# Rolled TensorE loops with loads counted on GpSimd, in a decode-step kernel (sliding-window attention beside an MLP)

## The chip, the cores and the metric

The kernel runs on one core of a Trainium2 chip. The metric is device time in microseconds (us) of one execution, the median of several runs. All times of the profile are in us from the start of the profiled span, if nothing else is said.

## The reference

One token (batch 1, one position, width 1024) goes through two branches whose results are added to the token. All tensors are bf16.

```python
x  = A_x
xn = layernorm(x)                                   # 1024 values
# A: attention of 32 heads in 4 groups over the last 4096 cached positions
q  = xn @ wq                                        # wq 1024 x 4096
scores = einsum(q, k_cache[:, :, -4096:]) * 128**-0.5
o  = softmax(scores) @ v_cache[:, :, -4096:]
a  = o @ wo                                         # wo 4096 x 1024
# B: MLP
h  = gelu(layernorm(xn) @ w1 + b1)                  # w1 1024 x 3584, tanh form
b  = h @ w2 + b2                                    # w2 3584 x 1024
out = x + a + b
```

Weights and cache together are 38 MB (of 2 to the 20 bytes): K and V 4 each, wq and wo 8 each, w1 and w2 7 each. Each is used once, by a single row of activations, so nearly all of the work is to bring them in.

## The kernel before

**Memory.** Each matrix lies in SBUF with 128 partitions. `WA` holds wq and later w2 and the end of wo; `W1` holds w1 and later most of wo; `KV` holds K and later V; `KT` is K transposed in blocks of 32 x 32 by DVE. So w2 can be loaded once q has been computed, V once K has been transposed, and wo once h has been computed.

**Loads.** SP (SyncE) issues all large transfers in one queue, in this order: four pieces of K (L212), wq in two halves of 4 MB, w1 in two halves of 3.5 MB (L152), then, after a wait on K's last transpose, four pieces of V (L266), after a wait on q (`done["q"]`) w2 in pieces of 16 and 12 rows, and after a wait on h (`done["h"]`) wo. A "row" of w2 or wo is here one matmul step: 128 partitions x 1024 columns, 256 KB. wo has 32 of them, in pieces of 10, 8, 6, 4, 2 and 1, with row 31 apart: eight small transfers (L275) put it into 64 partitions (`LOW`) between the second and the third piece.

**TensorE.** All its products have a single row of activations. The activations are the stationary operand (a window of a mostly zero tile, so that step number n writes into one PSUM row), the weights are the moving operand, 512 columns at a time. In order:

- the two layer norms' broadcast of x (L373);
- q: two loops, one for each half of wq, each with 8 rounds of 4 matmuls (`row_mms`, L379);
- the first half of h: 7 rounds of 4 (L379);
- the scores: 32 matmuls written out (L412), which need `QBD`, the transposed q that DVE makes in the meantime (copy L282, transpose L284, eight small copies L291);
- the second half of h, 7 rounds of 4. Meanwhile DVE and ScalarE make the maxima (L297), exp (L308) and the transposed probabilities (L312);
- h's transposes (L449), then the value product: 4 rounds of 8 (L454). Meanwhile gelu is computed on DVE and ScalarE;
- w2: a loop of 4 rounds of 8 for its first 16 rows (L464), four small matmuls that transpose the attention output (o2, L473), a loop of 3 rounds of 8 for the other 12 rows;
- wo, written out: rows 0 to 23 as pairs of matmuls, each half of the columns on its own 32-column tile of the array (L424); rows 24 to 30 as four matmuls of 256 columns on four tiles side by side (L430).

The first 24 rows' sums stand in two 32-row strips of one PSUM bank; ScalarE moves them (L357) into the bank in which the last rows add up. The two result halves are cast (L363) and written out.

Each loop is `pe.Fori`, a loop that the engine runs itself: addresses that depend on the index are computed by register instructions in TensorE's own instruction stream. For instance:

```python
            for k in rows:
                pe.matmul(bank(n), lhsT=vec[:, bass.ds(t + width * k, 128)], rhs=rhs_at(k, t), start=False, stop=False,
                          skip_group_check=True)
```

Matmul by matmul, one such address is `(index + constant) * 2 + base`.

## Time and profile before

| what | value |
|---|---|
| median of three runs | 101.78 us (100.42, 101.78, 102.19) |
| the profiled execution, its own time | 100.35 us |
| its span in the profile | 99.1 us |
| TensorE: matmuls, weight loads | 70.5 us busy, 341 matmuls |
| DMA read | 39.86 MB, 402 GB/s over the span |
| largest groups | q's 64 matmuls 17.9 us; the four K transposes on DVE 17.4; h's 56 matmuls 13.0; w2's 56 12.5; value product 8.5; scores 7.1 |

In the profile PE is TensorE's matmuls and PEld its weight loads, which run beside them. Register, branch and semaphore instructions are not counted as busy: where TensorE's sequencer works on them, the row says that the idle time ahead of the instruction is due to "issue". "x4" is the number of instructions that were put together in one row; the number in brackets is the idle time of the engine ahead of them, with what ended it. The slices are 2.48 us each, and a digit is the busy share in tenths.

### The profile page before, as it was taken

What the parts mean: (1) busy time and instruction counts of PE and PEld (TensorE: products, weight loads), DVE (VectorE), ACT (ScalarE), POOL (GpSimd) and SP (SyncE); (2) the same over time, 40 slices, a digit from 0 to 9 for tenths busy, and PEclk for the clock granted to TensorE, in tenths of its full rate; (3) what the DMA queues carried; (4) which work ended last, traced back from release to release, by engine and by line L of the source; (5) the groups of instructions that cost most, each with busy time, mean ns of one, the idle gap of its engine ahead of it and who ended that gap; (6) DMA issues with size and microseconds to landing.
All of it is one profiled execution on the core that took longest, in us unless ns stands there. A gap on an engine that the chain in (4) does not pass through costs nothing.

```text
span 99.1 us, 1197 instructions
## 1 busy us (share of the span) xinstructions
PE 70.5 (71%) x341; PEld 28.4 (29%) x341; DVE 37.5 (38%) x56; ACT 5.7 (6%) x11; POOL 6.5 (7%) x26
## 2 busy tenths in 40 slices
PE   0021000305999999999999999799999999979532
PEld 0000000002334433334444344233335445422210
DVE  0007998999999900091002543440024010000001
ACT  0500004200000000000000040000000000000021
POOL 6990000000000000000000000000000000000000
PEclk9999999999999999999999999999999999999996
DMA  2999999999999889889799999998999999999960
GB/s 26 397 426 418 430 436 436 489 476 463 450 423 397 370 382 544 370 382 544 301 423 420 423 522 423 423 423 370 476 476 422 388 397 427 423 402 440 397 256 4
DMA packets 3286, 39.89 MB, mean 402 GB/s; under 512 B 594, under 2 KB 596, under 8 KB 980
## 3 DMA queue, kind: packets, MB, share of 16 engines
q1 hardware_dynamic: 3076, 39.85, 95.0%
q10 hardware_dynamic: 208, 0.01, 0.1%
q8 instruction: 1, 0.02, 0.1%
q14 instruction: 1, 0.01, 0.0%
HBM read 39.86 MB, written 0.00 MB: 402 GB/s over the span
## 4 chain that ended last, share of the span: by engine, by line
DMA 46%; PE 40%; SPq 10%; issue 2%; DVE 0%
PE PS L379 31%; DMA WA<-in_A_wo_dram 26%; DMA WA<-in_A_wq_dram 20%; PE PS L412 7%; SPq L275 6%; SPq L152 2%; SPq L212 2%; PE PS L383 1%; PE PS L436 1%; DVE Pb L363 0%; PE PS L430 0%
## 5 line engine op out<-in xcount | busy, mean ns | idle before, releaser
L379 PE MATMUL PS<-WA,XZ 128*128 x64 | 17.9, 433 | 5.6 <-DMA WA<-in_A_wq_dram 5.2
L261 DVE STREAM_TRANSPOSE KT<-KV 128x4096 bf16<-128x4096 bf16 x4 | 17.4, 4409 | 0.0
L379 PE MATMUL PS<-W,YZ 128*128 x56 | 13.0, 381 | 0.0
L464 PE MATMUL PS<-WA,GT 128*64 x56 | 12.5, 380 | 0.0
L379 PEld LDWEIGHTS PS<-WA,XZ 128*128 x64 | 6.9, 108 | 17.0 <-issue 13.2
L383 PE MATMUL PS<-XBRP,HOT 1*128 1x512 bf16 x6 | 2.5, 454 | 9.5 <-DVE XZ L253 9.5
L454 PE MATMUL PS<-KV,PT 128*128 x32 | 8.5, 378 | 0.7 <-issue 0.7
L464 PEld LDWEIGHTS PS<-WA,GT 128*64 x56 | 6.0, 110 | 5.8 <-issue 1.2
L379 PEld LDWEIGHTS PS<-W,YZ 128*128 x56 | 5.2, 96 | 7.5 <-issue 2.5
L412 PE MATMUL PS<-KT,QBD 128*128 128x512 bf16 x32 | 7.1, 379 | 0.0
L424 PE MATMUL PS<-W,OT 128*32 128x512 bf16 x48 | 5.7, 380 | 1.8 <-DMA W<-in_A_wo_dram 1.8
L363 DVE CAST Pb<-PS 64x256 bf16<-64x256 f32 x1 | 0.4, 417 | 16.1 <-PE PS L430 16.1
L373 PE MATMUL PS<-XBRP,onesb 1*128 1x512 bf16 x2 | 1.0, 605 | 6.7 <-DMA XBRP<-in_B_b_dram 6.7
L297 DVE TENSOR_REDUCE MX<-PS 128x1 f32<-128x512 f32 x2 | 1.4, 692 | 10.0 <-PE PS L412 10.0
L454 PEld LDWEIGHTS PS<-KV,PT 128*128 x32 | 3.1, 96 | 6.1 <-issue 2.7
L223 DVE BATCH_NORM_STATS2 BN<-PS 128x6 f32<-128x512 f32 x2 | 1.3, 688 | 7.7 <-PE PS L373 7.7
L412 PEld LDWEIGHTS PS<-KT,QBD 128*128 128x128 bf16 x32 | 3.1, 98 | 3.7 <-issue 0.2
L383 PEld LDWEIGHTS PS<-XBRP,HOT 1*128 1x128 bf16 x6 | 0.5, 94 | 11.5 <-issue 11.5
L342 DVE SCALAR_TENSOR_TENSOR QBD<-PS,REC,GMASK 32x512 f32<-32x512 f32 x1 | 0.7, 739 | 7.9 <-PE PS L383 7.9
L424 PEld LDWEIGHTS PS<-W,OT 128*32 128x32 bf16 x48 | 2.1, 97 | 5.3 <-DMA W<-in_A_wo_dram 2.8
L282 DVE CAST Pb<-PS 128x512 bf16<-128x512 f32 x1 | 0.7, 692 | 7.4 <-PE PS L383 7.4
L308 ACT ACTIVATE Pb<-PS,NMB 128x1024 bf16<-128x1024 f32 x1 | 1.1, 1114 | 40.1 <-DVE NMB L305 40.1
(79 smaller groups left out, 33.4 us busy)
## 6 DMA issues: line engine op xcount, KB each, us to landing
WA<-in_A_wq_dram SPq DMA_DIRECT2D x2, 4096.0 KB, 24.4
W<-in_B_w_dram SPq DMA_DIRECT2D x2, 3584.0 KB, 41.0
KV<-in_A_k_cache_dram SPq DMA_DIRECT2D x4, 1024.0 KB, 7.9
KV<-in_A_v_cache_dram SPq DMA_DIRECT2D x4, 1024.0 KB, 20.6
WA<-in_B_w_dram SPq DMA_DIRECT2D x1, 4096.0 KB, 27.2
WA<-in_B_w_dram SPq DMA_DIRECT2D x1, 3072.0 KB, 34.2
W<-in_A_wo_dram SPq DMA_DIRECT2D x1, 2560.0 KB, 21.4
W<-in_A_wo_dram SPq DMA_DIRECT2D x1, 2048.0 KB, 25.9
```

What stands on the lines that cost most here:

```text
L152: sp.dma_start(dst[:, c0 * width:(c0 + n) * width].rearrange("p (c n) -> p c n", c=n), src[:, c0:c0 + n, :],).then_inc(semaphores[j], 16)
L212: sp.dma_start(KV[:, g * 4096:(g + 1) * 4096], A_k_cache[0, g, SK - W:SK, :].rearrange("(p i) d -> p (i d)", p=128)).then_inc(s_k[g], 16)
L223: DVE.mark(dve.bn_stats(out=BN[:, 12 * n + 6 * i:12 * n + 6 * i + 6], in_=src[:, 512 * i:512 * i + 512]))
L261: C["kt"] = DVE.mark(dve.transpose(KT[:, i * 4096:(i + 1) * 4096], KV[:, i * 4096:(i + 1) * 4096]))
L275: sp.dma_start(LOW[first:first + 29:4, :].rearrange("p (u n) -> p u n", u=2), low_source[first:first + 29:4]).then_inc(s_low, 16)
L297: DVE.mark(dve.tensor_reduce(out=MX2[:, b:b + 1], in_=S[:, 512 * b:512 * b + 512], axis=AX.X, op=ALU.max))
L379: pe.matmul(bank(n), lhsT=vec[:, bass.ds(t + width * k, 128)], rhs=rhs_at(k, t), start=False, stop=False, skip_group_check=True)
L383: return pe.matmul(bank(n), lhsT=HOT[:, 8:136], rhs=XB[0:1, 0:8, :], start=start, stop=not start, skip_group_check=True)
L412: last = pe.matmul(bank(3 + b), lhsT=QBD[:, g * 512 + j * 128:g * 512 + j * 128 + 128], rhs=K5[:, g, 16 * b:16 * b + 16, j, :], start=(n = ...
L424: ins = pe.matmul(acc(a), lhsT=window(vec, c, a), rhs=rhs[:, a * 512:(a + 1) * 512], start=False, stop=stop, tile_position=(0, 32 * a), sk ...
L454: pe.matmul(bank(1), lhsT=PT[:, bass.ds(i * 256 + u * 32, 128)], rhs=V4[:, :, bass.ds(i * 8 + u, 1), :], start=False, stop=False, skip_gro ...
L464: pe.matmul(bank(7, 64), lhsT=GT[:, bass.ds(i * (4 * STEP) + (LEAD + STEP * (c0 + u) - ROW - a), 64)], rhs=W2[:, bass.ds(i * 4 * D + ((c0 ...
```

## The change

- TensorE's loops are put together: q is one loop over both halves of wq around the loop of 8 rounds; h likewise, and as a whole after the scores; the scores are a loop of 4 rounds of 8; the value product is 8 rounds of 4; w2 is one loop of 7 rounds; wo's first 20 rows are a loop of 5 rounds, through the same code as w2, with matmuls of 128 stationary columns in place of the 64 (w2) and the tiled pairs (wo). [...]
- As one loop's body serves several loads, GpSimd waits for the loads in their order and counts one semaphore, `s_feed`, up; TensorE waits for it against a register, `turn`, that it adds one to in each round.
- w2's and wo's stationary tiles hold each vector twice, 64 columns apart, so that the sums come to stand in rows 31, 32, 95 and 96 of one bank, in which the last 12 rows add up too. ScalarE's move is gone.
- wo's row 31 is loaded as its last piece, not in eight small transfers; the pieces are now 8, 12, 8, 3 and 1 rows.
- K's fourth piece is issued after wq.
- The copy of q is done by ScalarE, and the eight small copies are shared by DVE and ScalarE.
- o2 stands after all of w2.

```diff
-WO_CHUNKS = [10, 8, 6, 4, 2, 1]
-WO_HEAD = 4
+WO_CHUNKS = [8, 12, 8, 3, 1]
+WO_HEAD = 2
-TAIL = 24
+TAIL = 20
+ROUND = 4
...
+    for semaphores, rounds in (
+            (s_wq, [1] * len(WQ_CHUNKS)), (s_w1, [1] * len(W1_CHUNKS)),
+            (s_w2, [n // ROUND for n in W2_CHUNKS]), (s_wo, [n // ROUND for n in WO_CHUNKS[:WO_HEAD]])):
+        for semaphore, n in zip(semaphores, rounds):
+            pool.wait_ge(semaphore, 16)
+            pool.sem_inc(s_feed, n)
...
+    for g in range(3):
+        load_k(g)
     load_chunks(WA, wq_p, WQ_CHUNKS, NQ, s_wq)
+    load_k(3)
     load_chunks(W1, w1_p, W1_CHUNKS, F, s_w1)
...
-    low_source = A_wo.rearrange("(u p j) n -> p u j n", u=2, j=32)[:, :, WO_MAIN, :]
-    for first in (0, 1, 2, 3, 32, 33, 34, 35):
-        sp.dma_start(
-            LOW[first:first + 29:4, :].rearrange("p (u n) -> p u n", u=2),
-            low_source[first:first + 29:4]).then_inc(s_low, 16)
...
-    DVE.mark(dve.tensor_copy(Q32, bank(7)))
+    act.wait_ge(done["q"], 16)
+    C["q32"] = ACT.mark(act.activation(out=Q32, in_=bank(7), func=ACTF.Copy))
...
-        dve.wait_ge(done["sc" if b else "sc0"], 1)
+        dve.wait_ge(done["sc"], 4)
...
-    C["d_GT"] = DVE.mark(dve.tensor_tensor(out=GT[:, LEAD:LEAD + STEP * FC:STEP], in0=HT[:, :], in1=U2[:, :], op=ALU.mult))
+    C["d_GT"] = DVE.mark(dve.tensor_tensor(
+        out=twice(GT, FC), in0=HT[:, :].unsqueeze(1).to_broadcast([128, 2, FC]),
+        in1=U2[:, :].unsqueeze(1).to_broadcast([128, 2, FC]), op=ALU.mult))
...
+    with pe.Fori(0, len(WQ_CHUNKS)) as j:
+        pe.wait_ge(s_feed, turn)
+        pe.reg_add(turn, turn, 1)
+        with pe.Fori(0, 8) as t:
+            for k in range(4):
+                last = add(bank(7), XZ[:, bass.ds(t + j * (4 * XW) + XW * k, 128)],
+                           WA[:, bass.ds(t * -512 + j * (4 * NQ) + (k * NQ + 7 * 512), 512)])
+            last.then_inc(done["q"], 1)
...
+    with pe.Fori(0, 4) as g:
+        for j in range(4):
+            for b in range(2):
+                last = add(bank(3 + b), QBD[:, bass.ds(g * 512 + j * 128, 128)],
+                           K4[:, bass.ds(g * 32 + 16 * b, 16), 32 * j:32 * j + 32])
+        last.then_inc(done["sc"], 1)
+
+    W1C = W1[:, :].rearrange("p (x c) -> p x c", c=4)
+    with pe.Fori(0, len(W1_CHUNKS)) as j:
+        pe.wait_ge(s_feed, turn)
+        pe.reg_add(turn, turn, 1)
+        with pe.Fori(0, 7) as t:
+            for k in range(4):
+                last = add(bank(0), YZ[:, bass.ds(t + j * 32 + 8 * k, 128)],
+                           W1C[:, bass.ds(t + j * F + k * (F // 4), 128, 7), :])
+            last.then_inc(done["h"], 1)
...
+    V3 = V.rearrange("p (g x) -> p g x", g=HKV)
+    with pe.Fori(0, 8) as i:
+        for u in range(4):
+            last = add(bank(1), PT[:, bass.ds(i * 128 + u * 32, 128)], V3[:, :, bass.ds(i * 512 + u * 128, 128)])
+        last.then_inc(done["pv"], 1)
+
+    def out_rounds(vec, weights, rows):
+        with pe.Fori(0, rows // ROUND) as i:
+            pe.wait_ge(s_feed, turn)
+            pe.reg_add(turn, turn, 1)
+            for u in range(ROUND):
+                for a in range(2):
+                    add(bank(7), vec[:, bass.ds(i * (2 * ROUND) + (LEAD + 2 * u - ROW - a), 128)],
+                        weights[:, bass.ds(i * (ROUND * D) + (u * D + a * 512), 512)])
+
     pe.wait_ge(DVE.sem, C["d_GT"])
+    out_rounds(GT, W2, FC)
     pe.wait_ge(DVE.sem, C["on"])
...
+    out_rounds(OT, W1, TAIL)
+
+    c0 = TAIL
+    for j, n in enumerate(WO_CHUNKS[WO_HEAD:]):
+        pe.wait_ge(s_wo[WO_HEAD + j], 16)
+        for c in range(c0, c0 + n):
+            rhs = (W1 if c < FC else WA)[:, c * D:(c + 1) * D]
+            for a in range(4):
+                first, column = LEAD + 2 * c - (0 if a % 2 else ROW), 7 * 512 + a // 2 * 256
+                last = add(PS[32 * a:32 * a + 32, column:column + 256], OT[:, first:first + 32],
+                           rhs[:, TAIL_AT[a]:TAIL_AT[a] + 256], tile_position=(0, 32 * a))
```

More of the change, by code (lines that the diff above doesn't have):

```diff
@@ L23 @@
 W2_CHUNKS = [16, 12]
-WO_CHUNKS = [10, 8, 6, 4, 2, 1]
-WO_HEAD = 4
-WO_LOW = 18
+WO_CHUNKS = [8, 12, 8, 3, 1]
+WO_HEAD = 2
 XW = 136
@@ L29 @@
 XP = 72
-TAIL = 24
+TAIL = 20
 TAIL_AT = [0, 512, 256, 768]
 ROW = 31
-STEP = 2
 LEAD = 32
-GW = 2 * LEAD + STEP * FC
-WO_MAIN = 31
+COPY = 64
+GW = 192
+ROUND = 4
 class Track:
@@ L74, in bass_parallel_sum__sliding_block_cached__mixer_channel_mlp__decode_kernel @@
     s_x, s_b1, s_v, s_out = (nc.alloc_semaphore(n) for n in ("s_x", "s_b1", "s_v", "s_out"))
-    s_low = nc.alloc_semaphore("s_low")
     s_w1 = sems("s_w1", len(W1_CHUNKS))
@@ L85, in bass_parallel_sum__sliding_block_cached__mixer_channel_mlp__decode_kernel @@
     done = {n: nc.alloc_semaphore(f"S_PE_{n}") for n in (
-        "x", "h", "hT", "q", "sc0", "sc", "pv", "tot", "o2", "rest", "fin")}
+        "x", "h", "hT", "q", "sc", "pv", "tot", "o2", "fin")}
+    s_feed = nc.alloc_semaphore("S_FEED")
     def sb(name, shape, d):
@@ L99, in bass_parallel_sum__sliding_block_cached__mixer_channel_mlp__decode_kernel @@
     HOT = sb("HOT", [1, 8 + 128], bf16)
-    EDGE = sb("EDGE", [2, 2 * LEAD + 1], bf16)
+    EDGE = sb("EDGE", [2, 132], bf16)
     XBRP = sb("XBRP", [2, 16 * XP], bf16)
@@ L127, in bass_parallel_sum__sliding_block_cached__mixer_channel_mlp__decode_kernel @@
     ON = sb("ON", [32, DH], bf16)
-    OT = sb("OT", [128, 2 * LEAD + 33], bf16)
+    OT = sb("OT", [128, GW], bf16)
     ONM = QBD[0:32, 0:1024].bitcast(f32)
@@ L132, in bass_parallel_sum__sliding_block_cached__mixer_channel_mlp__decode_kernel @@
     W1 = sb("W1", [128, KC * F], bf16)
-    LOW = KT[0:64, 0:2 * D]
     WA = sb("WA", [128, KC * NQ], bf16)
@@ L191, in bass_parallel_sum__sliding_block_cached__mixer_channel_mlp__decode_kernel @@
         fill=1.0, base=0, channel_multiplier=1))
-    POOL.mark(pool.memset(EDGE[:, LEAD:LEAD + 1], 1.0))
+    POOL.mark(pool.memset(EDGE[:, LEAD:LEAD + COPY + 1:COPY], 1.0))
     POOL.mark(pool.affine_select(
@@ L209, in bass_parallel_sum__sliding_block_cached__mixer_channel_mlp__decode_kernel, with load_k @@
     C["consts"] = POOL.cnt
-    for g in range(HKV):
+    for semaphores, rounds in (
[4 more added lines that the diff above has]
+            pool.sem_inc(s_feed, n)
+    def load_k(g):
         sp.dma_start(
@@ L268, in bass_parallel_sum__sliding_block_cached__mixer_channel_mlp__decode_kernel @@
             A_v_cache[0, g, SK - W:SK, :].rearrange("(p i) d -> p (i d)", p=128)).then_inc(s_v, 16)
-    sp.wait_ge(done["q"], 1)
+    sp.wait_ge(done["q"], 16)
     load_chunks(W2, w2_p, W2_CHUNKS, D, s_w2)
-    sp.wait_ge(done["h"], 1)
-    load_chunks(W1, wo_p, WO_CHUNKS[:2], D, s_wo)
-    low_source = A_wo.rearrange("(u p j) n -> p u j n", u=2, j=32)[:, :, WO_MAIN, :]
-    for first in (0, 1, 2, 3, 32, 33, 34, 35):
-        sp.dma_start(
-            LOW[first:first + 29:4, :].rearrange("p (u n) -> p u n", u=2),
-            low_source[first:first + 29:4]).then_inc(s_low, 16)
-    load_chunks(W1, wo_p, WO_CHUNKS[2:WO_HEAD], D, s_wo[2:], WO_LOW)
-    load_chunks(WA, wo_p, WO_CHUNKS[WO_HEAD:], D, s_wo[WO_HEAD:], FC)
-    dve.wait_ge(done["q"], 1)
-    DVE.mark(dve.tensor_copy(Q32, bank(7)))
+    sp.wait_ge(done["h"], 14)
+    load_chunks(W1, wo_p, WO_CHUNKS[:3], D, s_wo)
+    load_chunks(WA, wo_p, WO_CHUNKS[3:], D, s_wo[3:], FC)
+    act.wait_ge(done["q"], 16)
+    C["q32"] = ACT.mark(act.activation(out=Q32, in_=bank(7), func=ACTF.Copy))
+    dve.wait_ge(ACT.sem, C["q32"])
+    C["qtb"] = DVE.mark(dve.transpose(QTB, Q32))
     dve_wait()
-    DVE.mark(dve.transpose(QTB, Q32))
-    dve_wait()
+    act.wait_ge(DVE.sem, C["qtb"])
     dve.wait_ge(POOL.sem, C["consts"])
+    act.wait_ge(POOL.sem, C["consts"])
     QD = QBD[:, :].rearrange("p (g w) -> p g w", g=HKV)[:, :, 0:512].rearrange("p g (e b h) -> p g e b h", e=4, b=4)
@@ L290, in bass_parallel_sum__sliding_block_cached__mixer_channel_mlp__decode_kernel, with twice @@
         for u in range(2):
-            C["d_QBD"] = DVE.mark(dve.tensor_copy(
-                QD[32 * b:32 * b + 32, :, :, b, 4 * u:4 * u + 4], QS[32 * b:32 * b + 32, u:8:2, :, :]))
+            to, of = QD[32 * b:32 * b + 32, :, :, b, 4 * u:4 * u + 4], QS[32 * b:32 * b + 32, u:8:2, :, :]
+            if b < 2:
+                C["d_QBD"] = DVE.mark(dve.tensor_copy(to, of))
+            else:
+                C["a_QBD"] = ACT.mark(act.activation(out=to, in_=of, func=ACTF.Copy))
+    def twice(vec, n):
+        return vec[:, LEAD:LEAD + 2 * COPY].rearrange("p (u x) -> p u x", u=2)[:, :, 0:2 * n:2]
     S = PS[:, 3 * 512:5 * 512]
     for b in range(2):
-        dve.wait_ge(done["sc" if b else "sc0"], 1)
+        dve.wait_ge(done["sc"], 4)
         DVE.mark(dve.tensor_reduce(out=MX2[:, b:b + 1], in_=S[:, 512 * b:512 * b + 512], axis=AX.X, op=ALU.max))
@@ L312, in bass_parallel_sum__sliding_block_cached__mixer_channel_mlp__decode_kernel @@
     C["d_pt"] = DVE.mark(dve.transpose(PT[:, 0:1024], Pb[:, :]))
-    dve.wait_ge(done["h"], 1)
+    dve.wait_ge(done["h"], 14)
     C["d_h8"] = DVE.mark(dve.tensor_copy(H8, bank(0, 8)))
@@ L319, in bass_parallel_sum__sliding_block_cached__mixer_channel_mlp__decode_kernel @@
         out=HT[:, :].rearrange("p (t c) -> p c t", c=4),
-        in0=PS[:, 6 * 512:6 * 512 + 32].rearrange("p (c t) -> p c t", c=4)[:, :, 0:7],
+        in0=PS[:, 2 * 512 + 32:2 * 512 + 64].rearrange("p (c t) -> p c t", c=4)[:, :, 0:7],
         in1=B1T[:, :].rearrange("p (t c) -> p c t", c=4), op=ALU.add))
@@ L340, in bass_parallel_sum__sliding_block_cached__mixer_channel_mlp__decode_kernel @@
     dve_wait()
-    dve.wait_ge(done["pv"], 1)
+    dve.wait_ge(done["pv"], 8)
     DVE.mark(dve.scalar_tensor_tensor(
@@ L350, in bass_parallel_sum__sliding_block_cached__mixer_channel_mlp__decode_kernel @@
     dve.wait_ge(done["o2"], 1)
-    DVE.mark(dve.tensor_copy(OT[:, LEAD:LEAD + 32], PS[:, 2 * 512:2 * 512 + 32]))
     C["OT"] = DVE.mark(dve.tensor_copy(
-        OT[0:64, LEAD + WO_MAIN + 1:LEAD + WO_MAIN + 2], PS[64:128, 2 * 512 + WO_MAIN:2 * 512 + WO_MAIN + 1]))
-    act.wait_ge(done["rest"], 1)
-    for a in range(2):
-        C["rest"] = ACT.mark(act.activation(
-            out=PS[64 * a:64 * a + 64, 6 * 512:6 * 512 + 256], in_=PS[0:64, 7 * 512 + 256 * a:7 * 512 + 256 * a + 256],
-            func=ACTF.Copy))
+        twice(OT, 32), PS[:, 2 * 512:2 * 512 + 32].unsqueeze(1).to_broadcast([128, 2, 32])))
     for engine, track, a in ((act, ACT, 1), (dve, DVE, 0)):
         engine.wait_ge(done["fin"], 1)
-        of, to = PS[64 * a:64 * a + 64, 6 * 512:6 * 512 + 256], Pb[0:64, 256 * a:256 * a + 256]
+        of, to = PS[64 * a:64 * a + 64, 7 * 512 + 256 * a:7 * 512 + 256 * a + 256], Pb[0:64, 256 * a:256 * a + 256]
         track.mark(act.activation(out=to, in_=of, func=ACTF.Copy) if a else dve.tensor_copy(to, of))
@@ L374, in bass_parallel_sum__sliding_block_cached__mixer_channel_mlp__decode_kernel @@
     last.then_inc(done["x"], 1)
-    def row_mms(n, vec, width, rows, t_count, rhs_at):
-        with pe.Fori(0, t_count) as t:
-            for k in rows:
-                pe.matmul(bank(n), lhsT=vec[:, bass.ds(t + width * k, 128)], rhs=rhs_at(k, t), start=False, stop=False,
-                          skip_group_check=True)
-    def edge(n, start):
-        return pe.matmul(bank(n), lhsT=HOT[:, 8:136], rhs=XB[0:1, 0:8, :], start=start, stop=not start,
-                         skip_group_check=True)
@@ L386, in h_cols, with edge, add @@
-    def h_cols(row, t):
-        return row.rearrange("p (m a c) -> p m a c", m=128, a=7)[:, :, bass.ds(t, 1), :]
+    def edge(n):
+        pe.matmul(bank(n), lhsT=HOT[:, 8:136], rhs=XB[0:1, 0:8, :], start=True, stop=False, skip_group_check=True)
+    def add(to, lhsT, rhs, **place):
+        return pe.matmul(to, lhsT=lhsT, rhs=rhs, start=False, stop=False, skip_group_check=True, **place)
+    turn = pe.alloc_register("turn")
+    pe.reg_mov(turn, 1)
     pe.wait_ge(POOL.sem, C["hot"])
+    for n in (7, 3, 4):
+        edge(n)
@@ L390, in bass_parallel_sum__sliding_block_cached__mixer_channel_mlp__decode_kernel @@
     pe.wait_ge(DVE.sem, C["xz"])
-    edge(0, True)
-    edge(7, True)
+    edge(0)
+    edge(1)
     pe.wait_ge(POOL.sem, C["consts"])
-    k0 = 0
-    for j, n in enumerate(WQ_CHUNKS):
-        pe.wait_ge(s_wq[j], 16)
-        row_mms(7, XZ, XW, range(k0, k0 + n), 8, lambda k, t: WA[:, bass.ds(t * -512 + (k * NQ + 7 * 512), 512)])
-        k0 += n
-    edge(7, False).then_inc(done["q"], 1)
-    def h_rows(j):
-        pe.wait_ge(s_w1[j], 16)
-        k0 = sum(W1_CHUNKS[:j])
-        row_mms(0, YZ, 8, range(k0, k0 + W1_CHUNKS[j]), 7, lambda k, t: h_cols(W1[:, k * F:(k + 1) * F], t))
@@ L406, in bass_parallel_sum__sliding_block_cached__mixer_channel_mlp__decode_kernel @@
-    h_rows(0)
-    pe.wait_ge(DVE.sem, C["d_QBD"])
-    K5 = KT[:, :].rearrange("p (g i j k) -> p g i j k", g=HKV, i=32, j=4)
-    for b in range(2):
-        for n in range(16):
-            g, j = n // 4, n % 4
-            last = pe.matmul(bank(3 + b), lhsT=QBD[:, g * 512 + j * 128:g * 512 + j * 128 + 128],
-                             rhs=K5[:, g, 16 * b:16 * b + 16, j, :], start=(n == 0), stop=(n == 15))
-        last.then_inc(done["sc" if b else "sc0"], 1)
-    def acc(a):
-        return bank(7, 32, 32 * a)
@@ L418, in window @@
-    def window(vec, c, a):
-        first = LEAD + c - (0 if a else ROW)
-        return vec[:, first:first + 32]
-    def out_row(vec, c, rhs, stop=False):
-        for a in range(2):
-            ins = pe.matmul(acc(a), lhsT=window(vec, c, a), rhs=rhs[:, a * 512:(a + 1) * 512],
-                            start=False, stop=stop, tile_position=(0, 32 * a), skip_group_check=True)
-        return ins
-    def tail_row(vec, c, rhs, stop):
-        for a in range(4):
-            ins = pe.matmul(PS[32 * a:32 * a + 32, 6 * 512:6 * 512 + 256], lhsT=window(vec, c, a % 2),
-                            rhs=rhs[:, TAIL_AT[a]:TAIL_AT[a] + 256], start=False, stop=stop, tile_position=(0, 32 * a),
-                            skip_group_check=True)
-        return ins
+    with pe.Fori(0, len(WQ_CHUNKS)) as j:
[6 more added lines that the diff above has]
+            last.then_inc(done["q"], 1)
@@ new lines, in bass_parallel_sum__sliding_block_cached__mixer_channel_mlp__decode_kernel @@
+    pe.wait_ge(DVE.sem, C["d_QBD"])
+    pe.wait_ge(ACT.sem, C["a_QBD"])
+    K4 = KT[:, :].rearrange("p (x k) -> p x k", k=128)
+    with pe.Fori(0, 4) as g:
[13 more added lines that the diff above has]
+            last.then_inc(done["h"], 1)
@@ L435, in bass_parallel_sum__sliding_block_cached__mixer_channel_mlp__decode_kernel @@
+    pe.wait_ge(ACT.sem, C["exp"])
     for a in range(2):
-        pe.matmul(bank(7, 64), lhsT=EDGE[:, 1 - a:1 - a + 64], rhs=XB[:, 8 * a:8 * a + 8, :], start=(a == 0), stop=False,
+        pe.matmul(bank(7), lhsT=EDGE[:, 1 - a:129 - a], rhs=XB[:, 8 * a:8 * a + 8, :], start=(a == 0), stop=False,
                   skip_group_check=True)
-    h_rows(1)
-    edge(0, False).then_inc(done["h"], 1)
-    pe.wait_ge(ACT.sem, C["exp"])
     pe.matmul(PS[0:32, 5 * 512 + 129:5 * 512 + 130], lhsT=B32[:, :], rhs=SUMP[:, :]).then_inc(done["tot"], 1)
-    pe.wait_ge(DVE.sem, C["d_pt"])
@@ L444, in bass_parallel_sum__sliding_block_cached__mixer_channel_mlp__decode_kernel @@
-    pe.wait_ge(s_v, 64)
-    V4 = V.rearrange("p (g i d) -> p g i d", g=HKV, i=32)
     pe.wait_ge(DVE.sem, C["d_h8"])
     for c in range(4):
-        last = pe.matmul(PS[:, 6 * 512 + 8 * c:6 * 512 + 8 * c + 8], lhsT=H8[:, c:512:4], rhs=FLIP[:, :])
+        last = pe.matmul(PS[:, 2 * 512 + 32 + 8 * c:2 * 512 + 40 + 8 * c], lhsT=H8[:, c:512:4], rhs=FLIP[:, :])
     last.then_inc(done["hT"], 1)
-    edge(1, True)
-    with pe.Fori(0, 4) as i:
-        for u in range(8):
-            pe.matmul(bank(1), lhsT=PT[:, bass.ds(i * 256 + u * 32, 128)], rhs=V4[:, :, bass.ds(i * 8 + u, 1), :],
-                      start=False, stop=False, skip_group_check=True)
@@ L456, in bass_parallel_sum__sliding_block_cached__mixer_channel_mlp__decode_kernel @@
-    edge(1, False).then_inc(done["pv"], 1)
-    pe.wait_ge(DVE.sem, C["d_GT"])
-    def w2_loop(j):
-        pe.wait_ge(s_w2[j], 16)
-        c0 = sum(W2_CHUNKS[:j])
-        with pe.Fori(0, W2_CHUNKS[j] // 4) as i:
-            for u in range(4):
-                for a in range(2):
-                    pe.matmul(bank(7, 64),
-                              lhsT=GT[:, bass.ds(i * (4 * STEP) + (LEAD + STEP * (c0 + u) - ROW - a), 64)],
-                              rhs=W2[:, bass.ds(i * 4 * D + ((c0 + u) * D + a * 512), 512)],
-                              start=False, stop=False, skip_group_check=True)
@@ L469, in bass_parallel_sum__sliding_block_cached__mixer_channel_mlp__decode_kernel @@
-    pe.matmul(PS[:, 6 * 512:6 * 512 + 256], lhsT=HOT[:, 8:136], rhs=XB[0:1, 0:4, :], start=True, stop=True)
-    w2_loop(0)
+    pe.wait_ge(s_v, 64)
+    V3 = V.rearrange("p (g x) -> p g x", g=HKV)
[11 more added lines that the diff above has]
+                        weights[:, bass.ds(i * (ROUND * D) + (u * D + a * 512), 512)])
@@ L475, in bass_parallel_sum__sliding_block_cached__mixer_channel_mlp__decode_kernel @@
     last.then_inc(done["o2"], 1)
-    w2_loop(1)
     pe.wait_ge(DVE.sem, C["OT"])
-    c0 = 0
-    for j, n in enumerate(WO_CHUNKS):
-        if c0 == WO_LOW:
-            pe.wait_ge(s_low, 8 * 16)
-            for u in range(2):
-                out_row(OT[0:64, :], WO_MAIN + u, LOW[:, u * D:(u + 1) * D])
-        pe.wait_ge(s_wo[j], 16)
-        if c0 == TAIL:
-            pe.wait_ge(ACT.sem, C["rest"])
+    out_rounds(OT, W1, TAIL)
+    c0 = TAIL
+    for j, n in enumerate(WO_CHUNKS[WO_HEAD:]):
+        pe.wait_ge(s_wo[WO_HEAD + j], 16)
         for c in range(c0, c0 + n):
             rhs = (W1 if c < FC else WA)[:, c * D:(c + 1) * D]
-            last = out_row(OT, c, rhs, c == TAIL - 1) if c < TAIL else tail_row(OT, c, rhs, c == WO_MAIN - 1)
-        if c0 + n == TAIL:
-            last.then_inc(done["rest"], 1)
+            for a in range(4):
+                first, column = LEAD + 2 * c - (0 if a % 2 else ROW), 7 * 512 + a // 2 * 256
+                last = add(PS[32 * a:32 * a + 32, column:column + 256], OT[:, first:first + 32],
+                           rhs[:, TAIL_AT[a]:TAIL_AT[a] + 256], tile_position=(0, 32 * a))
         c0 += n
```

## The prediction, made before the changed kernel ran

> **What bounds the kernel now.** I read the 40 slices first, then the DMA queues, then the order of time around the loops, and last the end of the transfers.

> ```profile
> span 99.1 us, 1197 instructions
> PE 70.5 (71%) x341; PEld 28.4 (29%) x341; DVE 37.5 (38%) x56; ACT 5.7 (6%) x11; POOL 6.5 (7%) x26
> DMA  2999999999999889889799999998999999999960
> q1 hardware_dynamic: 3076, 39.85, 95.0%
> q8 instruction: 1, 0.02, 0.1%
> DMA 46%; PE 40%; SPq 10%; issue 2%; DVE 0%
> ```

> The 16 DMA engines are busy from slice 2 to slice 39: 39.85 MB in 95.0% of 99.1 us, 423 GB/s. So transfers set the end. The SPq in the chain is not a cost: wo's first piece is issued at 62.69, but w2's last piece, ahead of it in the queue, lands at 76.56. TensorE only has to keep up, and its reserve is small:

> ```profile
> 86.12 2.33 PE L424 MATMUL PS<-W,OT 128*32 128x512 bf16 x20
> 89.01 1.91 PE L424 MATMUL PS<-W,OT 128*32 128x512 bf16 x16 [0.56 <-DMA W<-in_A_wo_dram]
> 92.70 1.47 PE L424 MATMUL PS<-W,OT 128*32 128x512 bf16 x12 [1.25 <-DMA W<-in_A_wo_dram]
> 97.08 0.29 PE L430 MATMUL PS<-WA,OT 128*32 128x256 bf16 x4 [0.24 <-DMA WA<-in_A_wo_dram]
> ```

> It waits for wo's rows only from 88.45 on. The first ten, in since 84.05, it takes at 0.23 us a row, which is how it catches up. The second thing to see is the pace of its loops:

> ```profile
> 35.14 0.59 PEld L379 LDWEIGHTS PS<-WA,XZ 128*128 x4 [0.52 <-issue]
> 36.26 0.55 PEld L379 LDWEIGHTS PS<-WA,XZ 128*128 x4 [0.52 <-issue]
> 37.35 0.55 PEld L379 LDWEIGHTS PS<-WA,XZ 128*128 x4 [0.54 <-issue]
> ...
> 44.59 0.59 PEld L379 LDWEIGHTS PS<-W,YZ 128*128 x4 [0.35 <-issue]
> 45.60 0.55 PEld L379 LDWEIGHTS PS<-W,YZ 128*128 x4 [0.42 <-issue]
> 46.62 0.56 PEld L379 LDWEIGHTS PS<-W,YZ 128*128 x4 [0.46 <-issue]
> ...
> 66.25 2.12 PE L454 MATMUL PS<-KV,PT 128*128 x8 [0.24 <-issue]
> 68.61 2.16 PE L454 MATMUL PS<-KV,PT 128*128 x8 [0.24 <-issue]
> ...
> 75.30 1.45 PEld L464 LDWEIGHTS PS<-WA,GT 128*64 x8 [0.28 <-issue]
> 77.05 1.43 PEld L464 LDWEIGHTS PS<-WA,GT 128*64 x8 [0.29 <-issue]
> ```

> One round of q (4 matmuls) takes 1.10 us, of h 1.01, of the value product (8) 2.36, of w2 (8) 1.74. Matmuls from a written-out list come every 0.216 us (0.86 for 4, 1.73 for 8). So three of the four loops go at the pace of TensorE's sequencer, not of its array. The trace's records of register instructions say why. A matmul with two addresses from a loop index needs, for each address, add a constant, times 2 bytes, add the base: six operations, one fused instruction, and such a matmul takes 0.152 us of sequencer. A seventh operation (a slice along a strided dimension multiplies once more, as V4's does) is an instruction of its own: 0.245 us. The loop's end costs 0.097 + 0.266, a second fused instruction ahead of the first matmul 0.137.

> **The change, part by part.** Times are on the clock of this execution.

> *Loads.* Without K's fourth megabyte (pieces land 2.5 us apart), wq's halves land at 20.4 and 30.1, not 22.88 and 32.60. K's last lands at 32.6, its 4.41 us transpose ends at 37.0 (before: 34.62), and V is issued then; w1 fills the queue to 49.6, so this costs nothing; on SP two issues (wq's, 1.02) pass one (K's, 0.8). The bytes are the same. Without the eight pieces of wo's row 31 SP saves 5.8 us of issuing that the full queue hid. But they used half of the DMA engines: of wo's last piece, seven engines land by 95.6 and nine at 96.7 to 97.03, and DMA's share is 0.57 at 95 to 96. Spread evenly the end comes 0.6 to 0.8 earlier. That is all that the transfers can give.

> *Counting on GpSimd.* A wait and an increment there before TensorE sees a landing: between 0.05 (a semaphore record) and 0.23 (GpSimd's wait ahead of identb's select); I take 0.1. Nothing else is queued on GpSimd.

> *q.* One loop now holds both indices j and t. Two more scalings and two more adds make the head 12 operations, two full fused instructions in place of 6 + 2: 1.13 a round. The first half hides behind the slow matmuls after the idle time; the second: 30.1 + 0.5 + 8 x 1.13 + 0.4 = 40.0 (before: 42.0).

> *From q to the scores.* Before, half of h covered this (41.94 to 48.65). Now TensorE waits: ScalarE's copy 0.62 (between 0.38 for 256 columns and 1.11 for 1024), transpose 0.71, four small copies on each engine 0.9 (DVE's eight took 1.43; ScalarE's between 0.20 and 0.36 each), handovers 0.2: 2.45. Behind its copies ScalarE has only exp, not due before 53, so nothing there is held up. Scores at w2's pace of operations or less: 7.0, end 49.5. If their addresses take seven operations, +2.4. The maxima wait for both banks (+0.7), but exp is then done near 55 and TensorE wants it at 70.

> *h.* All 14 rounds now stand after the scores, with two indices and a step-7 slice on a view of stride 4: times 4, times 2, two adds, and three for the weights make seven. Round: 1.13 + 3 x 0.093 = 1.41. With 0.3 + 0.75 for starts: 14 x 1.41 + 1.05 = 20.8, end 70.3. Before, h's two halves took 13.1. Bounds: 14.1 + 1 if no operation is added, 20.8 as counted. I take the count: the strided slice of V4 is the nearest row and shows it. wo is issued 7.7 us later than before, at 70.4; w2's transfers cover that until 76.6.

> *Value product.* DVE's cast of h and the four small transposes as before: 1.15. V3's slice loses the seventh operation, but a round holds four: 8 x 1.08 = 8.65 (before 9.2), end 80.1.

> *w2.* 7 rounds of 1.74 plus a wait on a register. No row shows one; between nothing (folded into the next instruction) and 0.2 (wait and add apart); I take 0.11, nearest to the semaphore records (0.05, and 0.08 to 0.1 to the next instruction), with the add folded into the head's half-empty second instruction. 7 x 1.85 + 0.35 = 13.3, end 93.4. Weights of 128 columns for 64: the rows differ by 1 ns in the matmul (381, 380), nothing.

> *o2* stood between w2's halves, now after both: 0.26 + DVE 0.2 + handovers and loop start 0.75 = 1.2, start of wo at 94.6. All of its first rows are long in.

> *wo's 20 rows* run as w2 does, not as tiled pairs: 5 x 1.85 + 0.2 = 9.45, at 104.05, where before 20 rows took some 4.7 plus waits. The last 12 rows: start 0.3, then 0.11 a row (four tiles side by side at 95.19) and 0.28: 1.8. The sums end at 105.85, not 97.4. No moved row: ScalarE's 0.73 at 94.22 lay in a wait for DMA, nothing. The two casts and the output transfer stay.

> Sum: 97.40 to 105.85 is +8.45; on the execution's own time, 100.35 + 8.45 = **108.8**. The median of the runs shown is 1.4 above that execution; as the wait for transfers goes, I do not carry the 1.4 over (with it 110.2).

> **Code blocks.** A 16 KB code packet travels at 76.70 and takes 1.08 us on one DMA engine; wo's first two pieces then land 1.4 us later on one engine than on the rest (82.66 and 84.05, 87.58 and 88.97). No round of a loop is longer there: w2's stay at 1.74. [...]

> **Rivals.**

> *TensorE keeps up (not slower).* If the address work is folded, so that h runs at 0.9 a round and w2 and wo at 1.73, TensorE's chain is 40.0 + 2.45 + 7.0 + 13.5 + 1.15 + 7.2 + 12.4 + 1.2 = 84.9, earlier than the 86.1 of before. wo's rows 8 to 19 land near 90, 24 matmuls take 5.2, and the rest follows the transfers: 100.35 - 0.7 = 99.6. It decides where the chain loses under 3 us to address work. Against it: q's and h's rounds today, which exceed 0.86 with fewer operations.

> *Fewer operations than I count.* No seventh in h (-3.9) and a free wait (-1.3): 108.8 - 5.2 = 103.6. For it: equal subexpressions are shared today; against it, V4's row.

> *Slow clock after the new pause.* After 5.2 us idle, q's first matmuls came every 0.426 (weight loads at 24.20, 24.62, 25.05), 13 of them, 2.7 us lost. If 2.45 us idle does the same to the scores: 111.5. For it: the same array, the same cause. Against it: 1.2 us idle at 62.3 left the next matmuls fast. [...]

> **How the numbers follow.** My forecast 0.55, with its own range of 106.5 to 110.5; fewer operations 0.15 (103.6, between 102.5 and 106); slow clock 0.10 (111.5); TensorE keeps up 0.20 (99 to 102, with 0.03 for under 99.7). The median of before is 101.78; 2% of it, about what a measurement of this kernel can tell from no change, reaches from 99.7 to 103.8. So faster 0.03, the same 0.22 (0.17 and a third of the fewer-operations case), slower 0.75. The range leaves out the case in which TensorE keeps up: 102.8 to 111.6.

> **What would show it.** Right: pauses of the order of 0.5 us between groups of four in h, rounds near 1.41, h's end near 70, w2's end near 93, and no wait for DMA in wo; the DMA row empty for some 8 us before the end, since transfers still end near 96.4. Wrong: rounds of h near 0.9, or waits for wo's rows at the end: then the time is near 99.6, and the step that failed is the count of operations.

## The result, and the profile after

| | before | after |
|---|---|---|
| median of six runs each | 101.19 us (100.40 to 102.19) | 110.44 us (110.01 to 110.58) |
| profiled execution, its own time | 100.35 | 110.01 |
| its span | 99.1 | 108.3 |
| last landing of a weight | 97.03 | 96.40 |
| start of the last casts (sums complete) | 97.42 | 106.59 |

The changed kernel takes 1.095 times as long (95% interval 1.088 to 1.102): slower. The six executions of before fall into two groups, three near 100.5 and three near 102, and the factor leaves out the two above 101.9; the two medians alone would give 1.091. The page of after:

```profile
span 108.3 us, 1366 instructions
PE 78.1 (72%) x347; PEld 30.7 (28%) x347; DVE 36.0 (33%) x50; ACT 6.6 (6%) x14; POOL 6.7 (6%) x26
DMA  3999999999899999999999899999999999920000
q1 hardware_dynamic: 2740, 39.85, 86.9%
q8 instruction: 1, 0.02, 0.1%
PE 69%; DMA 17%; issue 8%; ACT 1%; DVE 1%; SPq 1%; POOLq 0%
```

The same 39.85 MB come at the same pace (86.9% of 108.3 us and 95.0% of 99.1 are both 94.1 us of the 16 engines), but the last five slices (2.71 us each) of the DMA row are almost empty. The transfers no longer set the end; in the chain PE has 69% where it had 40%, with most of DMA's 46% gone. The order of time of TensorE shows where it lies (start, duration, and in brackets the idle time ahead):

```profile
33.15 1.04 PE L387 MATMUL PS<-WA,XZ 128*128 x4 [0.24 <-issue]
...
44.62 8.61 PE L387 MATMUL PS<-KT,QBD 128*128 x32 [2.90 <-ACT QBD L300]
...
57.41 1.14 PE L387 MATMUL PS<-W,YZ 128*128 x4 [0.33 <-issue]
58.87 1.12 PE L387 MATMUL PS<-W,YZ 128*128 x4 [0.33 <-issue]
...
73.36 8.67 PE L387 MATMUL PS<-KV,PT 128*128 x32
82.13 12.86 PE L387 MATMUL PS<-WA,GT 128*128 x56
94.92 0.26 PE L457 MATMUL PS<-ON,E 32*128 32x32 bf16 x4
95.91 10.19 PE L387 MATMUL PS<-W,OT 128*128 x72 [0.73 <-DVE OT L364]
105.93 0.61 PE L387 MATMUL PS<-WA,OT 128*32 128x256 bf16 x16
```

From 73 on there is no wait for DMA in it. wo, whose rows are all in at 96.40, is taken from 95.91 to 106.54. And the weight loads of w2 show the pace of its rounds, 1.81 to 1.82 us from start to start (before: 1.75):

```profile
83.97 1.41 PEld L387 LDWEIGHTS PS<-WA,GT 128*128 x8 [0.43 <-issue]
85.78 1.41 PEld L387 LDWEIGHTS PS<-WA,GT 128*128 x8 [0.40 <-issue]
```

### The profile page after: what moved, and what is told of

Read it like the earlier page. It is cut to its first block, busy times and chain, and to the rows that moved or that the text cites. A ratio compares the mean times of both kernels' runs of the same rounds, so it can differ in the third digit from the quotient of the medians.

```text
span 108.3 us, 1366 instructions
## 1 busy us (share of the span) xinstructions
PE 78.1 (72%) x347; PEld 30.7 (28%) x347; DVE 36.0 (33%) x50; ACT 6.6 (6%) x14; POOL 6.7 (6%) x26
## 3 DMA queue, kind: packets, MB, share of 16 engines
q1 hardware_dynamic: 2740, 39.85, 86.9%
## 4 chain that ended last, share of the span: by engine, by line
PE 69%; DMA 17%; issue 8%; ACT 1%; DVE 1%; SPq 1%; POOLq 0%
PE PS L387 68%; DMA WA<-in_A_wq_dram 17%; SPq L217 1%; ACT QBD L300 1%; DVE PT L287 1%; ACT Pb L285 1%; PE PS L429 1%; DVE Pb L370 0%; DVE OT L364 0%; PE PS L434 0%; PE PS L457 0%; PE PS L431 0%; POOLq L214 0%
## 5 line engine op out<-in xcount | busy, mean ns | idle before, releaser
L387 PE MATMUL PS<-W,YZ 128*128 x56 | 15.2, 381 | 4.0 <-issue 3.9
L387 PE MATMUL PS<-WA,GT 128*128 x56 | 12.9, 380 | 0.1
L387 PEld LDWEIGHTS PS<-WA,XZ 128*128 x64 | 7.0, 109 | 16.9 <-issue 13.3
L387 PE MATMUL PS<-W,OT 128*128 (+1 forms) x72 | 10.2, 333 | 0.7 <-DVE OT L364 0.7
L387 PE MATMUL PS<-KT,QBD 128*128 x32 | 8.6, 437 | 2.9 <-ACT QBD L300 2.9
L387 PEld LDWEIGHTS PS<-WA,GT 128*128 x56 | 5.4, 97 | 7.5 <-issue 3.1
L387 PEld LDWEIGHTS PS<-W,OT 128*128 (+1 forms) x72 | 4.6, 97 | 6.1 <-issue 2.9
L387 PEld LDWEIGHTS PS<-KT,QBD 128*128 x32 | 3.5, 110 | 8.0 <-issue 5.3
L325 DVE CAST H<-PS 8x512 bf16<-8x512 f32 x1 | 0.7, 678 | 13.6 <-PE PS L387 13.6
```

What stands on the lines that cost most here:

```text
L325: C["d_h8"] = DVE.mark(dve.tensor_copy(H8, bank(0, 8)))
L387: return pe.matmul(to, lhsT=lhsT, rhs=rhs, start=False, stop=False, skip_group_check=True, **place)
```

## The experiments

The theory was that of the prediction: TensorE's sequencer, with its address work, became the bound, above all in h (a seventh operation and two indices) and in wo (a loop of wide matmuls for written-out tiled pairs). The rivals: GpSimd's counting and the waits on it, the slow clock after the new pause, and the order of h and the scores. Each kernel was timed beside before on its own chip; before's medians there were 100.41, 100.57 and 100.52 in the three sets. After was not timed again in them, so that "below after" compares medians of different sets; after's own six executions lie within 0.6. Where an expectation counts to the 256th instruction of TensorE's code, it takes that for the border of a code block; this was my assumption, and no run shows it (see `halves_const`).

**h with a constant half** (`h_const`): two loops written one after the other, weights sliced as before.

```diff
-    with pe.Fori(0, len(W1_CHUNKS)) as j:
+    for j in range(2):
...
-                last = add(bank(0), YZ[:, bass.ds(t + j * 32 + 8 * k, 128)],
-                           W1C[:, bass.ds(t + j * F + k * (F // 4), 128, 7), :])
+                last = add(bank(0), YZ[:, bass.ds(t + 8 * k, 128)], h_cols(W1[:, k * F:(k + 1) * F], t))
```

> The changed kernel with h as two loops of 7 rounds whose half of w1 is a constant, so that an address needs three operations again and a round of four matmuls four fused instructions, nothing else. If TensorE's sequencer sets the chain (my theory): h's rounds fall from 1.47 us to 1.01, h ends 6 us earlier (near 66.3 in place of 72.3), and the time falls by 6.0, from 110.4 to 104.4. If the time were lost to the pause and the slow clock ahead of the scores, or to counting loads on GpSimd, h would still end about then but by the array's own pace: less than 2 us off.

Measured 103.71, ratio to before 1.034 (1.030 to 1.039): 6.7 below after. Weight loads of h:

```profile
54.10 0.60 PEld L387 LDWEIGHTS PS<-W,YZ 128*128 x4 [0.28 <-issue]
55.12 0.56 PEld L387 LDWEIGHTS PS<-W,YZ 128*128 x4 [0.41 <-issue]
```

A round takes 1.02 in the first half, as in before, and 1.10 in the second, whose head has a second fused instruction. h ends at 65.91 in place of 72.26, and the sums are complete 6.2 earlier. The address work in h is real and is on the path to the end.

**h with six operations** (`six_ops`): both indices stay, only the slice is taken along the contiguous dimension (W1 padded by 28 columns).

```diff
...
+                columns = W1[:, bass.ds(t * 4 + j * (4 * F) + k * F, F)]
                 last = add(bank(0), YZ[:, bass.ds(t + j * 32 + 8 * k, 128)],
-                           W1C[:, bass.ds(t + j * F + k * (F // 4), 128, 7), :])
+                           columns.rearrange("p (m a c) -> p m a c", m=128, a=7)[:, :, 0, :])
```

> The changed kernel with h's weights addressed by column number (slice of 3584 columns from t*4 + j*14336 + k*3584, then viewed in steps), so that a matmul's addresses take six operations in place of seven; both indices and the order stay. My theory: 3 single register instructions of 0.093 us go from each of 14 rounds, a round falls from 1.47 to 1.19, h ends 3.9 us earlier: 106.5. If the second index is what costs, and the seventh operation is hidden, the time stays within 1 us of 110.4.

Measured 106.53, 1.059 (1.053 to 1.064), 3.9 below after:

```profile
61.69 0.59 PEld L387 LDWEIGHTS PS<-W,YZ 128*128 x4 [0.61 <-issue]
62.90 0.56 PEld L387 LDWEIGHTS PS<-W,YZ 128*128 x4 [0.61 <-issue]
```

1.19 to 1.21 a round for 1.47: the three seventh operations cost 0.28, that is 0.093 each. The second index in the head costs another 0.17 against the first half of `h_const`, and 0.1 against the second.

**wo written out as narrow tiles** (`wo_tiles`): all 32 rows as four matmuls of 256 columns side by side.

```diff
-WO_HEAD = 2
+WO_HEAD = 0
-TAIL = 20
+TAIL = 0
...
-    out_rounds(OT, W1, TAIL)
```

> The changed kernel with all 32 rows of wo written out as four 256-column matmuls on four tiles side by side, as its last 12 rows are, with direct waits on wo's pieces; the code then passes its 256th instruction in wo's row 10. My theory: all rows but a few have landed when wo starts at 95.9, a row takes 0.11 us in place of 0.456, so wo's sums end 6.9 us earlier, near 99.7: 103.5. If passing the end of the code block under way costs a stall, wo ends later than that by the stall, visible as a pause between its rows.

Measured 102.49, 1.020 (1.018 to 1.022), 8.0 below after:

```profile
95.40 3.24 PE L387 MATMUL PS<-W,OT 128*32 128x256 bf16 x112 [0.32 <-DVE OT L364]
98.47 0.61 PE L387 MATMUL PS<-WA,OT 128*32 128x256 bf16 x16
```

All 128 matmuls take 3.7 us where after takes 10.6 for the same rows. It is the dearest part of the change: before could catch up in wo, after cannot.

**Half of h ahead of the scores** (`h_first`): each half a loop of its own, the first one ahead of the scores.

```diff
...
+    h_half(0)
...
     with pe.Fori(0, 4) as g:
...
-    with pe.Fori(0, len(W1_CHUNKS)) as j:
...
+    h_half(1)
```

> The changed kernel with h's first half ahead of the scores again, in the time in which q is transposed; seven operations per matmul stay (the step-7 slice), only one index goes. My theory: the pause of 2.9 us is filled, the scores start near 50.9 instead of 44.6 and run at 0.216 us, h's second half ends 4.7 us earlier than now: 105.7. If the sequencer's total work alone counts, and the pause was hidden by it, the gain is only that of the removed index, 1.3 us: 109.1.

Measured 105.08, 1.046 (1.044 to 1.047), 5.4 below after. h's first half runs from 41.89 to 50.69, beside the copies of q, and the scores follow it with no pause but 0.34. This run changes two things at once; by the rounds, the order was worth the 2.9 of the pause, and the rest (rounds of 1.25 to 1.40 for 1.47) came from the single index.

**No wait per round** (`no_round_waits`): w2's and wo's loops wait once for all of their loads.

```diff
...
-    def out_rounds(vec, weights, rows):
+    def out_rounds(vec, weights, rows, landed):
+        for semaphore in landed:
+            pe.wait_ge(semaphore, 16)
         with pe.Fori(0, rows // ROUND) as i:
-            pe.wait_ge(s_feed, turn)
-            pe.reg_add(turn, turn, 1)
...
```

> The changed kernel with the waits of w2 and of wo's 20 rows taken out of the rounds: each loop waits directly for its two pieces ahead of its first round, and GpSimd counts only wq and w1. My theory: a round falls from 1.82 to 1.74 us, twelve rounds gain 1.0 us: 109.4. If counting on GpSimd is what slows the loops, the gain is several us: below 107.

Measured 108.86, 1.083 (1.082 to 1.085), 1.6 below after:

```profile
85.48 1.44 PEld L386 LDWEIGHTS PS<-WA,GT 128*128 x8 [0.29 <-issue]
87.18 1.47 PEld L386 LDWEIGHTS PS<-WA,GT 128*128 x8 [0.26 <-issue]
```

The weight loads of a round now start every 1.70, so wait and add cost the sequencer 0.12 of 1.82. The matmuls of a round come every 1.73, the array's own pace (8 x 0.216), so that a round gains 0.09 and the 12 rounds some 1.0, as expected; in the two traces the sums are complete 1.1 earlier. GpSimd's counting is a small part, not the cause.

**A warm array** (`warm`): 12 idle matmuls, whose sums nobody reads, in the pause ahead of the scores.

```diff
+    pe.wait_ge(s_w1[0], 16)
+    for n in range(12):
+        pe.matmul(bank(6), lhsT=YZ[:, 0:128], rhs=W1[:, 0:512], start=True, stop=True, skip_group_check=True)
```

> The changed kernel with 12 matmuls of no use (into a bank that nothing reads) in the pause ahead of the scores; they use the first half of w1, which has landed. The scores then run at the full clock, 0.216 us a matmul in place of 0.426 for the first eight. By the rival of the slow clock the time falls by 1.7 us, to 108.7. By my theory the array is not the limit: the sequencer is through with the scores' instructions at 50.7 either way and h's rounds follow its pace, so h ends within 0.4 us of where it ends now, and the time stays at 110.4.

Measured 111.15, 1.104 (1.096 to 1.112), 0.7 above after:

```profile
41.76 2.76 PE L409 MATMUL PS<-W,YZ 128*128 128x512 bf16 x12
44.75 7.08 PE L387 MATMUL PS<-KT,QBD 128*128 x32 [0.23 <-issue]
```

The scores are 1.5 faster and nothing comes of it: h ends at 72.67. By then the sequencer sets the end. `wo_tiles` shows the same without the edit: there the scores happened to take 7.08, yet h ended at 72.15, against 72.26 with after's 8.61. In after the sequencer was through with the scores at 50.65, 2.6 before the array, and h's first 16 matmuls came from its queue every 0.25. Of the 1.1 by which `warm`'s sums are later than after's, 0.5 are there when wo starts, and 0.6 arise in wo: its rounds take 1.95 on average (by the starts of its weight loads) in place of 1.82. I put that to the 24 added instructions, which by my count move wo's loop over the border of a code block (code comes in a packet of 16 KB, at 76.70 in before and at 105.68 in after); no run shows it by itself.

The remaining kernels ask what an end set by transfers is worth, since after's change of the loads (no small pieces of row 31) and of the code (its packet at 105.68 in place of 76.70) could have gained something there.

**Before with row 31 as part of the last pieces** (`row31_last`):

```diff
-WO_CHUNKS = [10, 8, 6, 4, 2, 1]
+WO_CHUNKS = [10, 8, 6, 4, 3, 1]
-WO_MAIN = 31
+WO_MAIN = 32
-    for first in (0, 1, 2, 3, 32, 33, 34, 35):
-        sp.dma_start(
...
```

> The kernel before with wo's row 31 as the last of a three-row piece's successors (pieces of 10, 8, 6, 4, 3 and 1 rows) in place of the eight small loads, nothing else. If the eight small loads alone made some DMA engines late, all engines land wo's last piece together and the end comes 0.6 to 0.8 us earlier: ratio 0.993. My theory: the 16 KB code packet near 76.7 still holds one engine up by 1.4 us, so that one engine lands the last piece last, near 97.4, and the time does not move: ratio 0.998 to 1.002.

Measured 101.00, 1.002 (0.999 to 1.006): no change. The code packet travels at 76.80. A landing is counted up in 16 steps; of the last piece the first comes at 95.99, the fifteenth at 96.54 and the sixteenth, alone, at 97.74, as if one of the 16 engines were late:

```profile
95.27 0.62 PE L419 MATMUL PS<-W,OT 128*32 128x256 bf16 x16 [1.01 <-DMA W<-in_A_wo_dram]
97.14 1.04 PE L419 MATMUL PS<-WA,OT 128*32 128x256 bf16 x16 [1.25 <-DMA WA<-in_A_wo_dram]
```

**After with all constant halves** (`halves_const`): q and h as two loops each with a constant half, h's first half ahead of the scores; wo's loop stays.

```diff
-    with pe.Fori(0, len(WQ_CHUNKS)) as j:
+    for j in range(2):
...
+    h_half(0)
     with pe.Fori(0, 4) as g:
...
+    h_half(1)
```

> The changed kernel with q's and h's loops made for one half each (one index, six operations), and h's first half ahead of the scores; the loops still end at instruction 230, inside the first 256. My theory: h's second half ends near 61.6, the value product near 71.4, w2 near 84.4, wo's loop starts near 85.4 and waits for its rows, and the end follows the transfers, with the code packet only near 96: fin near 96.8, 99.8 us, ratio 0.99 to the kernel before. If the counted waits or the 128-column matmuls cost more than their rounds show, wo's loop ends after 95 and the time stays over 101.

Measured 101.83, 1.010 (1.004 to 1.017): a miss by 2.0.

```profile
86.63 10.81 PE L387 MATMUL PS<-W,OT 128*128 x72 [0.76 <-DVE OT L364]
97.28 0.61 PE L387 MATMUL PS<-WA,OT 128*32 128x256 bf16 x16
```

TensorE was 9.3 earlier at wo than in after (at 86.63; 85.4 was expected). But wo's rounds took 1.84 to 2.09, on average 1.95, its loop lasted until after 96, and the sums were complete at 97.88 without a wait for DMA on the way: TensorE still ended last, the case, though not for the cause, that the expectation names for a time over 101. I put the longer rounds, as in `warm`, to the border of the code block, over which the added instructions carried the loop. The packet came at 91.14, with data still to come, and the last piece landed from 95.91 to 97.49, so that a faster loop alone would not have brought the sums' end before 97.8. I had put the border at instruction 256 of the program's own code, and the runs put it earlier: after's wo loop, which by the trace's records ends near instruction 190, keeps its 1.82; that of `warm`, 24 further on, and this one, which by the expectation ends at 230, do not. Near 210 is my estimate from these three.

**The same with the scores written out** (`halves_scores_out`), to move the packet to an earlier time:

```diff
-    with pe.Fori(0, 4) as g:
+    for g in range(4):
```

> As halves_const, with the 32 matmuls of the scores written out as in the kernel before, so that the 256th instruction falls inside wo's loop. If code blocks matter only through their packet: it travels near 86, one DMA engine lands wo's last pieces 1 to 1.4 us later, and the time is 0.6 to 1.3 us above halves_const. If a loop across the boundary stalls on each taken branch, wo's five rounds show it as longer than 1.82 us each. If neither: the same as halves_const within 0.3.

Measured 101.30, 1.004 (1.000 to 1.008), 0.5 below `halves_const` instead of above: a miss too. The packet came at 77.22 and the last piece landed from 95.99 to 98.23. Both kernels have a packet ahead of the last data, so the pair holds no contrast, and it settles nothing about the packet. It does show something of the loops: here the packet comes during w2's loop, whose rounds take 1.89 on average, and wo's loop, behind the border, is back at 1.80, but for one round that takes 2.42 where a piece lands late (90.82).

**Both repairs together.** `six_ops_tiles` joins `six_ops` and `wo_tiles`; `h_const_tiles` has `h_const`'s h instead, and `halves_tiles` `halves_const`'s q and h, each with wo as in `wo_tiles`. The two latter have more loop code, and the packet comes earlier (93.03 and 88.76 against 95.55); TensorE is earlier at wo in both (89.16 and 86.26 against 91.86).

> six_ops and wo_tiles together. wo's list then starts near 91.5, passes the block's end (by the runs so far near instruction 210 of the program) near 92, and the code packet travels near 95.5, when its DMA engine has nearly done. My theory: all engines land the last piece together near 96.4, wo's sums end near 96.8, and the time is 100.1, 0.3 under the kernel before. If the packet takes its engine's time whenever it comes, the last piece lands near 97.5 on one engine: 101.2.

> h_const and wo_tiles together: TensorE is 2.4 us ahead of six_ops_tiles, but the code packet travels near 93, while its engine still has data to bring. My theory: that engine lands the last piece near 97.5, and the time is 101.0 to 101.3, 1 us slower than six_ops_tiles although TensorE is earlier. If only TensorE's own chain counts, it is equal or faster: 100.1 or less.

> halves_const and wo_tiles together: TensorE starts wo near 86.5, as early as the kernel before, and passes the block's end near 87; the packet travels near 90.5. My theory: as h_const_tiles, the last piece lands near 97.5 on one engine: 101.0 to 101.3. If what kept halves_const from 99.8 was wo's loop and not the packet, this is 100.1 or less.

| kernel | median | ratio to before | wo starts | packet | last piece lands |
|---|---|---|---|---|---|
| `six_ops_tiles` | 100.22 | 0.995 (0.991 to 0.999) | 91.86 | 95.55 | 95.93 to 97.73 |
| `h_const_tiles` | 101.41 | 1.008 (1.006 to 1.011) | 89.16 | 93.03 | 95.97 to 97.55 |
| `halves_tiles` | 101.42 | 1.008 (1.006 to 1.011) | 86.26 | 88.76 | 95.84 to 97.56 |

Of these three, the kernel in which TensorE is latest has the best median, and it is the only one of all whose median lies below before's (by 0.3, too little to call it faster). The profiled execution of `six_ops_tiles` was not one of the typical ones: it took 101.46, while eight of its twelve runs lie between 100.05 and 100.23 (two more at 101.31 and 101.58, one far off at 182.09). In that execution the packet still met the end of the transfers:

```profile
91.86 3.24 PE L387 MATMUL PS<-W,OT 128*32 128x256 bf16 x112 [0.32 <-DVE OT L364]
95.80 0.51 PE L387 MATMUL PS<-WA,OT 128*32 128x256 bf16 x12 [0.70 <-DMA WA<-in_A_wo_dram]
97.77 0.29 PE L387 MATMUL PS<-WA,OT 128*32 128x256 bf16 x4 [1.47 <-DMA WA<-in_A_wo_dram]
```

The last four matmuls wait 1.47 for a landing on one engine. `h_const_tiles`, 2.7 earlier at wo, waits there for rows and gains nothing:

```profile
89.16 2.37 PE L387 MATMUL PS<-W,OT 128*32 128x256 bf16 x80 [0.32 <-DVE OT L364]
95.23 1.90 PE L387 MATMUL PS<-W,OT 128*32 128x256 bf16 x32 [3.71 <-DMA W<-in_A_wo_dram]
```

The reading is that a packet which comes while data are on the way costs some 1.2 us at the end, and one which comes after them nothing. The steps of the landings bear it out. With the packet at 95.58 or later (after, `h_const`, `six_ops`, `wo_tiles`, `no_round_waits`, `warm`) the last piece is in at 96.26 to 96.48, its sixteenth step at most 0.22 behind the fifteenth. With the packet at 95.55 or earlier (`row31_last`, `h_first`, `halves_const`, `halves_scores_out` and the three of the table) that step comes 1.2 to 1.7 behind, at 97.49 to 98.23. And it is late only in pieces that land after the packet: in `six_ops_tiles` (packet at 95.55) in the last one, in `h_first` (94.98) in the last two, in `h_const_tiles` (93.03) in the last three. The packet of `h_const` did no harm although it came 0.8 ahead of the last landing; whether its engine had brought its share by then is not shown. The traces do not name the engine of a step, so that it is the one with the packet is inferred; no kernel moved the packet alone, and no typical run of `six_ops_tiles` has a trace.

The slow clock is no rival here. It was at 0.50 in `h_const_tiles` from 94.11 and in `halves_tiles` from 94.81 on, but there the sums are complete 0.45 after the last landing, against 0.34 in `six_ops_tiles`: it accounts for 0.1.

## Why the prediction was right, point by point

| step | predicted | measured in after |
|---|---|---|
| wq's halves land | 20.4, 30.1 | 20.59, 30.30 |
| a round of q; q's end | 1.13; 40.0 | 1.26; 41.74 |
| pause ahead of the scores | 2.45 | 2.88 |
| scores | 7.0 | 8.61 (the sequencer 6.3) |
| a round of h; h's end | 1.41; 70.3 | 1.47; 72.26 |
| value product's end | 80.1 | 82.03 |
| a round of w2; its end | 1.85; 93.4 | 1.82; 94.99 |
| start of wo | 94.6 | 95.91 |
| wo's 20 rows; last 12 | 9.45; 1.8 | 9.1; 1.5 |
| sums complete | 105.85 | 106.54 |
| last landing, earlier by | 0.6 to 0.8 | 0.63 |

- **The forecast's cause holds.** The end moved from the transfers to TensorE's sequencer: +9.2 in the span against +8.45 forecast, or 110.01 for 108.8 on the execution's own time. `h_const` and `wo_tiles` take most of it back, each by itself, and the two together (`h_const_tiles`) bring the end back to the transfers.
- **h: the count of operations was right.** `six_ops` isolates the seventh operation at 0.093, the value used.
- **q was the mis-sized term.** "Two full fused instructions in place of 6 + 2: 1.13 a round" took each fused instruction at one price. The records give 0.163 and 0.108 us for the two in q's head, where before's two take 0.078 and 0.042, and a round 1.26; which operations make them dearer no run isolates. At that pace the first half did not hide as the prediction has it: the sequencer was through with it only at 30.78, 0.5 after the second half had landed, and the turn of the outer loop up to the next matmul took another 1.1, where 0.5 was taken from the landing on. So the second half began at 31.87, not 30.6, and q ended 1.7 later than forecast. From there the error goes both ways: 2.2 at the start of the scores, 1.2 when the sequencer is through with them, 2.0 at h's end, 1.6 at w2's and 0.7 at the sums, since w2, o2 and wo were each a little cheaper than taken. That these partly cancel is luck.
- **The wait on a register** costs the sequencer 0.12 a round with its add, by `no_round_waits`, and the round 0.09; 0.11 was taken.
- **From q to the scores**: 0.43 more than taken. ScalarE's four copies took 1.03 us, not 0.9; DVE's four 0.68.
- **Spread of the transfers**: the last landing came earlier as forecast, and was worth nothing as long as TensorE was last. `row31_last` shows that the eight small pieces alone did not hold up before's end: without them a single step is late by about as much, by the reading above on the engine that carried the code packet.
- **The rival with the slow clock** came true in its mechanism and not in its price. The granted clock was 0.50 from 44.35 to 47.76, the scores took 1.5 longer than in `wo_tiles`, and h's end was the same within 0.1 (`wo_tiles`; in `warm` it came 0.4 later). The prediction added an array's loss to a sum that the sequencer sets.
- **The rival with fewer operations** is excluded by `six_ops`; that of a free wait by `no_round_waits`; that TensorE keeps up by the empty end of the DMA row.
- **Code blocks.** The forecast found no stall per round to save. `warm` and `halves_const`, whose wo loop by my count lies across the border, show a small one: 0.13 us a round (1.95 in place of 1.82). Each of the two traces shows one packet in all, not one a round, and no run shows what the rounds wait for there. What the loops put together did bring, a packet at 105.68 when no data are left, is worth nothing in after.

Not accounted for: of the 9.66 us by which the profiled execution grew, 0.5 lie outside the span. Own time less span is 1.25 in before and 1.29 in `row31_last`, but 1.6 to 1.7 in after and every kernel made from it. No run asked why.
